# Keys, queries and values read as rows of 6 KB and turned on VectorE; the first two triangular inverses as pairs of 16-blocks; the second group's norms and inverse planned inside the first Mlp

## The chip, the cores and the metric

One NeuronCore of a Trainium2 chip runs the whole program. The metric is the device time of one execution in microseconds. The engines are named as the profile names them: PE (TensorE matmul) and PEld (its weight loads), DVE (VectorE), ACT (ScalarE), POOL (GpSimd) and SP (SyncE, which here only issues DMAs). Every engine runs its own list of instructions strictly in order.

## The reference

A delta-rule attention over 32 heads (batch 4 times 8 heads, 768 tokens, head width 48), then two Mlps over the 3072 tokens, each 384 to 2048 to 384:

```
for t in range(S):                      # 768 steps, for all 32 heads
    y[t]  = q[t] @ state
    v_old = k_n[t] @ state              # k_n = k / (|k| + 1e-6)
    state = state + beta[t] * outer(k_n[t], v[t] - v_old)
x = y as 3072 x 384
x = rational(x @ moe_w_in)  @ moe_w_out     # P(h) / (Q(h) + 1e-6)
x = (h * tanh(softplus(h))) @ moe2_w_out    # h = x @ moe2_w_in
```

## The kernel before, in words

The sequence is cut into 24 chunks of 32 tokens (C = 32), and four chunks make a group (GU = 4), so there are six groups of 128 tokens for each of the 32 heads. One group gives 512 rows of x, which is one column block of the Mlps (TOK = 512).

For each group G the attention has these parts. `norms(G)` loads k of four chunks, squares it (ACT), sums it (DVE), takes the root (ACT, with Ln and Exp) and the reciprocal (DVE). `prepare(u)` scales k of chunk u, transposes k and q on PE, copies them (ACT), forms the Gram matrix (`gram`, PE), and masks it into `lg` (the strictly lower 32 x 32 matrix of each head) and `am`. `inverse(G)` turns the four `lg` tiles with one block transpose (`first`) and then solves for the inverse of a unit triangular 32 x 32 matrix for 128 (chunk, head) pairs at once: for j = 1 to 30 one multiply (L415) and one add (L421), 60 instructions in a row, each needing the one before. Group 0 does this on DVE, groups 1 to 5 on POOL (`ONPOOL`). `finish(G)` transposes the result back (`last`, L440) and scales it by beta into `xt` (L445). `step(u)` then runs the recurrence of chunk u: `ks` (L480), `rest`, `uu` (L492, the first to need `xt`), `s_mm` (L506), `y_mm` (L527), and the transposes that write x.

Each Mlp block (m, G) has 16 units f. A unit is nine matmuls of 512 columns into a bank h (`up`, L751), an activation chain, and nine matmuls into the banks o (`down`, L757). For m = 1 the chain has five DVE instructions (L790 to L796), seven on ACT and two or three on POOL (L785, L789, L798); for m = 2 it is two ACT instructions (Mish) and one on DVE (L802). The weights come as 64-bit floats; `convert` cuts each 384 KB piece to two 32-bit parts, on POOL (clamp L619, and L648 for the low part where kind has "p"), ACT, DVE and, for the first twelve f, on PE (L653, L654).

The order on every engine is made by the class `Plan`: each operation is given with a guessed duration, the buffers that it reads and writes, and a due time; a list scheduler picks, per engine, the ready operation with the earliest latest-start. `early=` moves an attention operation ahead by up to AHEADP = 100000 ns. The plan gets the operations in this order: group 0's attention, norms of group 1, the 16 units (1, 0) with the conversions, then prepares(1), finish(1), norms(2), then in turn the steps of group g + 1, units (2, g), the preparations of group g + 2 and g + 3, and units (1, g + 1).

## Time and profile before

| | us |
|---|---|
| median of 3 runs | 1147.59 (1145.57 to 1147.85) |
| the profiled execution | 1146.76 |
| its span, first to last instruction | 1145.0 |
| PE busy in that span | 1050.4 (92%) |
| DVE / ACT / POOL busy | 630.6 / 613.7 / 571.8 |

The span is the time from the first to the last instruction; 1.8 us of the execution lie around it. A busy share is a mean over stages that differ much: PE is nearly always busy from 452 us on, and it is the first 452 us that hold most of its idle time.

### The profile page before, as it was taken

What the parts mean: (1) busy time and instruction counts of PE and PEld (TensorE: products, weight loads), DVE (VectorE), ACT (ScalarE), POOL (GpSimd) and SP (SyncE); (2) the same over time, 40 slices, a digit from 0 to 9 for tenths busy, and PEclk for the clock granted to TensorE, in tenths of its full rate; (3) what the DMA queues carried; (4) which work ended last, traced back from release to release, by engine and by line L of the source; (5) the groups of instructions that cost most, each with busy time, mean ns of one, the idle gap of its engine ahead of it and who ended that gap; (6) DMA issues with size and microseconds to landing.
All of it is one profiled execution on the core that took longest, in us unless ns stands there. A gap on an engine that the chain in (4) does not pass through costs nothing.

```text
span 1145.0 us, 32730 instructions
## 1 busy us (share of the span) xinstructions
PE 1050.4 (92%) x13568; PEld 847.8 (74%) x13568; DVE 630.6 (55%) x1047; ACT 613.7 (54%) x1089; POOL 571.8 (50%) x741
## 2 busy tenths in 40 slices
PE   4858799569899988999999999999999999999997
PEld 4545587347678877778888788888777788889997
DVE  3784698627768843238762248852347668731211
ACT  2525798524578842248852268842257578742221
POOL 3201497896446996716678026785026457600000
PEclk8869999789999998999999999999999999999999
DMA  7665783737986764657676566766557556766773
GB/s 154 147 190 132 225 286 100 240 111 212 274 250 166 211 183 120 148 146 190 172 207 182 145 166 176 194 169 176 134 159 190 134 153 190 194 179 189 198 207 83
DMA packets 194228, 202.79 MB, mean 177 GB/s; under 512 B 126464, under 2 KB 139776, under 8 KB 194080
## 3 DMA queue, kind: packets, MB, share of 16 engines
q1 hardware_dynamic: 182304, 197.85, 62.8%
q10 hardware_dynamic: 11648, 2.76, 1.3%
q8 instruction: 107, 1.75, 0.7%
q14 instruction: 41, 0.34, 0.1%
q0 software_dynamic: 128, 0.10, 0.0%
HBM read 168.40 MB, written 29.88 MB: 173 GB/s over the span
## 4 chain that ended last, share of the span: by engine, by line
PE 75%; POOL 8%; DVE 5%; DMA 5%; ACT 3%; issue 3%; SPq 1%; ACTq 0%; DVEq 0%; POOLq 0%
PE b_h L751 31%; PE b_o L757 24%; PE b_o L766 4%; PE b_t L527 3%; POOL xs L421 3%; DMA arena<-in_moe_w_in_dram 3%; POOL tmp L415 3%; PE b_t L506 2%; PE b_t L492 2%; PE b_t L361 2%; PE b_t L480 2%; PE b_t L766 1%; PE b_t L349 1%; PE b_h L653 1%; DMA kn<-in_k_dram 1%
## 5 line engine op out<-in xcount | busy, mean ns | idle before, releaser
L751 PE MATMUL b_h<-x,win 128*128 128x512 f32 x1620 | 409.2, 397 | 12.8 <-ACT mq L801 9.7
L751 PEld LDWEIGHTS b_h<-x,win 128*128 128x128 f32 x1620 | 299.1, 189 | 80.3 <-ACT mq L801 10.3
L757 PE MATMUL b_o<-gh,wout 128*128 128x512 f32 x1332 | 335.4, 397 | 5.0 <-POOL wout L648 2.8
L757 PEld LDWEIGHTS b_o<-gh,wout 128*128 128x128 f32 x1332 | 246.2, 189 | 59.7 <-POOL wout L648 3.6
L802 DVE TENSOR_TENSOR gh<-mq,gh 128x512 fp32r<-128x512 f32 x96 | 71.9, 750 | 205.3 <-ACT mq L801 198.1
L800 ACT ACTIVATE gh<-b_h 128x512 fp32r<-128x512 f32 x96 | 57.4, 598 | 216.4 <-PE b_h L751 211.9
L789 POOL TENSOR_TENSOR mq<-mq,mr 128x512 f32<-128x512 f32 x96 | 124.3, 1295 | 79.8 <-ACT mr L787 75.2
L798 POOL TENSOR_TENSOR gh<-mq,gh 128x512 fp32r<-128x512 f32 x96 | 124.3, 1296 | 34.9 <-ACT gh L797 34.5
L421 POOL TENSOR_TENSOR xs<-xs,tmp 128x30 f32<-128x30 f32 (+9 forms) x150 | 84.4, 563 | 11.8
L794 DVE SCALAR_TENSOR_TENSOR mq<-mq,b_r 128x512 f32<-128x512 f32 x96 | 65.6, 683 | 44.7 <-ACT b_r L793 44.5
L790 DVE TENSOR_TENSOR ms<-ms,b_h 128x512 f32<-128x512 f32 x96 | 65.4, 681 | 37.5 <-ACT ms L788 36.8
L415 POOL TENSOR_TENSOR tmp<-xs 128x30 f32<-128x30 f32 (+9 forms) x150 | 78.5, 524 | 9.8
L619 POOL TENSOR_SCALAR arena<-arena 128x384 f32<-128x384 f32 x64 | 34.0, 533 | 98.5 <-PE b_h L653 58.0
L781 ACT ACTIVATE mr<-mq,cst 128x512 f32<-128x512 f32 x96 | 69.1, 720 | 19.2 <-POOL mq L789 18.4
L783 ACT ACTIVATE mq<-b_h 128x512 f32<-128x512 f32 x96 | 56.9, 592 | 41.1 <-PE b_h L751 39.7
L788 ACT ACTIVATE ms<-b_h,ab 128x512 f32<-128x512 f32 x96 | 73.9, 770 | 5.9 <-PE b_h L751 5.4
L791 DVE SCALAR_TENSOR_TENSOR ms<-ms,ab,b_h 128x512 f32<-128x512 f32 x96 | 71.7, 747 | 3.2
L795 DVE SCALAR_TENSOR_TENSOR b_r<-ms,ab,b_r 128x512 f32<-128x512 f32 x96 | 71.9, 749 | 0.0
L797 ACT CAST gh<-mq 128x512 fp32r<-128x512 f32 x96 | 58.8, 615 | 16.2 <-DVE mq L796 13.1
L796 DVE SCALAR_TENSOR_TENSOR mq<-mq,b_r 128x512 f32<-128x512 f32 x96 | 65.7, 685 | 2.5
L793 ACT ACTIVATE b_r<-mr 128x512 f32<-128x512 f32 x96 | 57.7, 601 | 2.8 <-DVE mq L796 1.5
L785 POOL TENSOR_SCALAR mr<-mq,ab 128x512 f32<-128x512 f32 x48 | 37.3, 776 | 40.9 <-ACT mq L783 40.3
(165 smaller groups left out, 1401.0 us busy)
## 6 DMA issues: line engine op xcount, KB each, us to landing
win<-wd SPq DMA_DIRECT2D x164, 384.0 KB
wout<-wd SPq DMA_DIRECT2D x164, 384.0 KB
arena<-in_moe_w_out_dram SPq DMA_DIRECT2D x32, 384.0 KB
wd<-x SPq DMA_DIRECT2D x24, 384.0 KB
wd<-win SPq DMA_DIRECT2D x16, 384.0 KB
wd<-wout SPq DMA_DIRECT2D x16, 384.0 KB
arena<-in_moe_w_in_dram SPq DMA_DIRECT2D x16, 384.0 KB
kn<-in_k_dram SPq DMA_DIRECT2D x88, 48.0 KB
```

What stands on the lines that cost most here:

```text
L415: eng.tensor_tensor(out=tv, in0=row[:, j, j + 1:C].unsqueeze(1).to_broadcast([128, j, n]), in1=xs[:, 0:j, j:j + 1].to_broadcast([128, j, n ...
L421: eng.tensor_tensor(out=xs[:, 0:j, j + 1:C], in0=xs[:, 0:j, j + 1:C], in1=tv, op=ALU.add)
L751: nc.tensor.matmul(out=h, lhsT=win[:, a, j], rhs=x[:, c, slab[j]], start=n == 0, stop=n == 8)
L757: nc.tensor.matmul(out=self.banks[f"o{d}"], lhsT=wout[:, a, d], rhs=gh[:, c], start=first and j == 0, stop=last and j == 2,)
L781: act(out=r, in_=q, func=ACTF.Ln, bias=k["c"])
L788: p.add("ACT", 775, lambda: act(out=s, in_=h, func=ACTF.Identity, scale=k["a3"], bias=k["a2"]), [hb], [sb])
L789: p.add("POOL", 1335, lambda: P.tensor_tensor(out=q, in0=q, in1=r, op=ALU.mult), [rb], [qb])
L791: p.add("DVE", 750, lambda: V.scalar_tensor_tensor(out=s, in0=s, scalar=k["a1"], in1=h, op0=ALU.add, op1=ALU.mult), [hb], [sb])
L795: p.add("DVE", 750, lambda: V.scalar_tensor_tensor(out=rp, in0=s, scalar=k["a0"], in1=rp, op0=ALU.add, op1=ALU.mult), [sb], ["r"])
L796: p.add("DVE", 690, lambda: V.scalar_tensor_tensor(out=q, in0=q, scalar=2.0, in1=rp, op0=ALU.subtract, op1=ALU.mult, reverse0=True), ["r"] ...
L798: p.add("POOL", 1320, lambda: P.tensor_tensor(out=gh[:, 1], in0=q, in1=gh[:, 0].bitcast(F32), op=ALU.subtract), [qb], [ghb])
L802: p.add("DVE", 755, lambda: V.tensor_tensor(out=gh[:, 1], in0=q, in1=gh[:, 0].bitcast(F32), op=ALU.subtract), [qb], [ghb])
```

## The change

- **Loads.** k, q and v of one group were 16 DMAs each, with runs of 192 bytes (one token of one head). They are now rows of 32 tokens (32 x 48 x 4 = 6 KB) of one head: four DMAs for k and q, two for v. The row lands in a staging tile with (head, chunk) on partitions, and one DVE transpose in blocks of 32 x 32 over 1536 columns (`turn`) puts tokens on partitions. There are three such turns per group. The staging tile is the one that holds outputs of the second Mlp (`ev`), and for later groups a part of the arena; k, q and v take it in turn. q and v share one tile, `qv`. The loads of group 0 are all issued by SP but for half of k; before, ACT issued half of k, and q and v.
- **Norms.** k is squared, summed and scaled in the staging tile, in one or two instructions over 1536 columns, before it is turned. The scaling is one instruction per group (DVE for group 0, POOL for the others).
- **Inverse of groups 0 and 1** (`HALVED`): the two diagonal 16 x 16 blocks are solved together in 14 steps (28 instructions of 28 to 112 elements, not 60 of 30 to 240). The lower left block is then added by `finish`: 128 small matmuls (`right`), an ACT copy, 128 small matmuls (`left`) and one DVE instruction, with one more DVE transpose of 512 columns beside them.
- **Place in the plan.** prepares(1), finish(1) and norms(2) are given to the plan at f = 6 of the first Mlp's 16 units, no longer behind them; norms and prepares of groups 3 to 5 at f = 2 of units (1, g + 1).
- **Smaller:** the exchange of k halves between partitions (`swap`) is two DMAs per group, not eight; `mb`, `y`, `kns` and the norm tiles have one buffer; `heat` multiplies the identity by itself; all four `mq` tiles hold q of group 0.

```
+HALVED = (0, 1)
...
+    def load(self, what, G, engines):
+        n = 128 // len(self.src[what])
+        for i, src in enumerate(self.src[what]):
+            engines[i % 2].dma_start(
+                out=self.staging(what, G)[0][n * i:n * i + n], in_=src[:, GU * C * G:GU * C * (G + 1)].rearrange("n (g t) d -> n g (t d)", g=GU)
+            )
+    def staging(self, what, G):
+        return self.stages[G >= (3 if what == "k" else 2)]
+    def turn(self, out, stage):
+        self.nc.vector.transpose(
+            out=out[:, :, :, 0:self.D].rearrange("p g m d -> p d m g"), in_=stage.rearrange("p t d -> p d t")
+        )
...
     def setup(self):
-        for u in range(GU):
-            self.load_k(u, nc.sync, (0, 1))
-            self.load_k(u, nc.scalar, (2, 3))
+        self.load("k", 0, (nc.sync, nc.scalar))
...
     def norms(self, p, G):
+        on, eng, ns = ("POOL", nc.gpsimd, 3300) if G else ("DVE", nc.vector, 1750)
+        p.add(
+            on, ns, lambda: eng.tensor_tensor(
+                out=stage, in0=stage, in1=w["ri"].unsqueeze(2).to_broadcast([128, C, D]), op=ALU.mult
+            ), [f"{wb}r"], staged, early=lead(AHEADX, G),
+        )
+        p.add("DVE", TURN, lambda: self.turn(kg, stage), staged, names, early=lead(AHEADX, G))
...
     def inverse(self, p, G):
+        nb = 2 if G in HALVED else 1
+        L = C // nb
-        for j in range(1, C - 1):
+        for j in range(1, L - 1):
...
     def finish(self, p, G):
+        if G in HALVED:
+            p.add("PE", 2000, right, names + [f"lg{g}" for g in range(GU)], ["t0"], early=lead(AHEADX, G))
+            p.add(
+                "ACT", 600, lambda: nc.scalar.activation(out=low, in_=bank, func=ACTF.Identity, scale=self.half),
+                ["t0"], [lowb], early=lead(AHEADX, G),
+            )
+            p.add("PE", 2000, left, [upb, lowb], ["t0"], early=lead(AHEADX, G))
...
     def first(f):
+        if f == 6:
+            at.prepares(plan, 1)
+            at.finish(plan, 1)
+            at.norms(plan, 2)
...
     units(1, 0, 0, first)
-    at.prepares(plan, 1)
-    at.finish(plan, 1)
-    at.norms(plan, 2)
     for g in range(NG - 2):
...
-        if g + 3 < NG:
-            at.norms(plan, g + 3)
-            at.prepares(plan, g + 3)
-        else:
+        if g + 3 == NG:
             at.steps(plan, g + 2)
-        units(1, g + 1, g + 2 == NG - 1)
+        units(1, g + 1, g + 2 == NG - 1, lambda f: prepare(g + 3) if f == 2 and g + 3 < NG else None)
```

The order of instructions on three engines shows what the plan makes of it.

ACT, from the program's start (L229, L235 and L241 load k, q and v; L303 squares k). Before:

```order
L229 DMA kn_148<-in_k_dram 32x8x48 x8
L892 ACTIVATE minus<-ident_144 128x128
L241 DMA v_151<-in_v_dram 32x8x48 x4
L235 DMA qn_149<-in_q_dram 32x8x48 x4
L303 ACTIVATE sq_171<-kn_148 128x384
```

Now (L234 loads, L340 squares, L354 takes the first half of the root):

```order
L234 DMA ev_134<-in_k_dram 32x1x1536 x2
L986 ACTIVATE minus<-ident_138 128x128
L1003 ACTIVATE ab<-ab 128x2
L340 ACTIVATE kn_142<-ev_134 128x16x48 x2
L717 ACTIVATE arena<-arena 128x384
L354 ACTIVATE nrm_1_167<-nrm_0_166 128x32
```

The loads of v and q have left ACT's list, and the first square stands behind two DMA issues instead of sixteen.

DVE, between the third `lg` of group 0 and the first steps of its inverse (L633 and L638 are weight conversion, L367 writes `lg`, L406 is `first`). Before:

```order
L367 TENSOR_TENSOR lg_172<-b_t_103,mb_165 128x256
L633 TENSOR_SCALAR b_r<-arena 128x384
L638 SCALAR_TENSOR_TENSOR arena<-arena,b_r 128x384
L633 TENSOR_SCALAR b_r<-arena 128x384
L638 SCALAR_TENSOR_TENSOR arena<-arena,b_r 128x384
L367 TENSOR_TENSOR lg_172<-b_t_103,mb_166 128x256
L406 STREAM_TRANSPOSE b_o<-lg_172 128x1024
L409 MEMSET b_o 128x32
```

Now, from the second `lg` on (L413 writes `lg`, L245 is a turn, L726 and L731 are weight conversion):

```order
L413 TENSOR_TENSOR lg_160<-b_t_103,mb_155 128x256
L245 STREAM_TRANSPOSE mq_122<-ev_134 128x48x8x4
L413 TENSOR_TENSOR lg_160<-b_t_103,mb_155 128x256
L726 TENSOR_SCALAR b_r<-arena 128x384
L731 SCALAR_TENSOR_TENSOR arena<-arena,b_r 128x384
L726 TENSOR_SCALAR b_r<-arena 128x384
L731 SCALAR_TENSOR_TENSOR arena<-arena,b_r 128x384
L413 TENSOR_TENSOR lg_160<-b_t_103,mb_155 128x256
L448 STREAM_TRANSPOSE b_o<-lg_160 128x1024
L451 MEMSET b_o 128x32
L453 MEMSET b_o 128x16x16
```

The turn of q stands between the second and the third `lg`; the turn of v stands three steps into the inverse, further down.

POOL, where the inverse of group 1 begins. Before, it comes behind the last L798 of units (1, 0), among the conversions for the second Mlp:

```order
L798 TENSOR_TENSOR gh_133<-mq_126,gh_133 128x512
L648 TENSOR_TENSOR x_114<-arena,x_114 128x384
L648 TENSOR_TENSOR win_115<-arena,win_115 128x384
L619 TENSOR_SCALAR arena<-arena 128x384 x2
L648 TENSOR_TENSOR wout_119<-arena,wout_119 128x384
```

(Eight rows further on in this list, L409 begins it.) Now it stands among the units; L884 and L893 are L789 and L798 of before, and 24 more rows of the inverse follow the four shown, before the next L893:

```order
L893 TENSOR_TENSOR gh_131<-mq_122,gh_131 128x512
L741 TENSOR_TENSOR x_113<-arena,x_113 128x384
L880 TENSOR_SCALAR mr_126<-mq_122,ab 128x512
L884 TENSOR_TENSOR mq_122<-mq_122,mr_126 128x512
L712 TENSOR_SCALAR arena<-arena 128x384
L451 MEMSET xs_161 128x32
L453 MEMSET xs_161 128x16x16
L468 TENSOR_TENSOR tmp_163<-xs_161 128x28
L474 TENSOR_TENSOR xs_161<-xs_161,tmp_163 128x2x14
L468 TENSOR_TENSOR tmp_163<-xs_161 128x52
L474 TENSOR_TENSOR xs_161<-xs_161,tmp_163 128x2x2x13
```

The whole inverse has moved in front of eight of the 16 L893 of units (1, 0).

## Rows read from the trace of the kernel before

**Rows 1.** The page, part 1: busy us (share) and count of each engine.

```profile
PE 1050.4 (92%) x13568; PEld 847.8 (74%) x13568; DVE 630.6 (55%) x1047; ACT 613.7 (54%) x1089; POOL 571.8 (50%) x741
```

**Rows 2.** Windows: us, then busy us of PE, PEld, DVE, ACT, POOL; PEclk, DMA share, GB/s.

```profile
0.00:117.40 117.40, 78.31 (x1967) 60.80 (x1968) 66.54 (x154) 46.52 (x104) 25.16 (x57) 0.84 0.64 158
117.40:205.00 87.60, 79.74 (x581) 62.86 (x580) 74.87 (x128) 72.95 (x136) 66.85 (x69) 0.98 0.67 203
205.00:260.00 55.00, 32.52 (x246) 24.17 (x246) 24.24 (x38) 21.07 (x38) 50.11 (x87) 0.81 0.51 172
260.00:327.00 67.00, 61.36 (x1423) 47.50 (x1421) 48.33 (x91) 37.77 (x78) 32.14 (x43) 1.00 0.82 246
420.00:452.00 32.00, 25.23 (x167) 20.02 (x167) 10.11 (x12) 7.70 (x14) 21.84 (x44) 0.89 0.48 132
452.00:1100.00 648.00, 642.57 (x8111) 523.14 (x8111) 330.23 (x510) 347.91 (x589) 301.58 (x356) 1.00 0.65 173
```

**Rows 3.** Timeline of ACT and its DMA queue (ACTq), opening: start, us, instruction, [idle before].

```profile
13.54 2.90 ACTq L235 DMA_DIRECT2D qn<-in_q_dram  x4
16.49 0.52 ACT L303 ACTIVATE sq<-kn 128x384 f32<-128x384 f32 x1 [9.03 <-DMA arena<-in_moe_w_in_dram]
...
47.36 0.52 ACT L624 ACTIVATE arena<-arena 128x384 f32<-128x384 f32 x1 [4.32 <-DMA mq<-in_q_dram]
```

**Rows 4.** Timeline of DVE, opening: from the scaled k to the inverse's end.

```profile
27.02 1.66 DVE L373 TENSOR_TENSOR kn<-kn,nrm 128x384 f32<-128x384 f32 x2
...
30.91 0.42 DVE L367 TENSOR_TENSOR lg<-b_t,mb 128x256 f32<-128x256 f32 x1
...
43.50 2.03 DVE L406 STREAM_TRANSPOSE b_o<-lg 128x1024 f32<-128x1024 f32 x1
...
48.98 0.18 DVE L415 TENSOR_TENSOR tmp<-xs,b_o 128x30 f32<-128x30 f32 x1
...
50.50 0.27 DVE L415 TENSOR_TENSOR tmp<-xs,b_o 128x108 f32<-128x108 f32 x1
...
72.50 1.89 DVE L440 STREAM_TRANSPOSE xt<-b_o 128x1024 f32<-128x1024 f32 x1
```

**Rows 5.** Timeline of PE: the first matmul on `xt`, and the first `up`.

```profile
74.91 1.34 PE L492 MATMUL b_t<-r,xt 32*32 32x48 f32 x56 [12.87 <-DVE xt L445]
...
117.42 2.22 PE L751 MATMUL b_h<-x,win 128*128 128x512 f32 x9
```

**Rows 6.** Timeline of POOL: first weight piece, and the inverse of group 1.

```profile
13.37 0.53 POOL L619 TENSOR_SCALAR arena<-arena 128x384 f32<-128x384 f32 x1 [2.77 <-DMA arena<-in_moe_w_in_dram]
...
213.17 0.24 POOL L415 TENSOR_TENSOR tmp<-xs 128x30 f32<-128x30 f32 x1
...
215.84 0.40 POOL L421 TENSOR_TENSOR xs<-xs,tmp 128x108 f32<-128x108 f32 x1
```

**Rows 7.** Timeline of PE in the same stretch.

```profile
226.25 3.95 PE L751 MATMUL b_h<-x,win 128*128 128x512 f32 x9 [8.60 <-ACT mq L801]
...
259.88 0.32 PE L492 MATMUL b_t<-r,xt 32*32 32x48 f32 x10
```

**Rows 8.** Groups by line: xcount, busy us, mean ns, idle before and its releasers.

```profile
L445 POOL TENSOR_TENSOR xt<-xt,beta_t 128x256 f32<-128x256 f32 x20 | 13.1, 687 | 85.8 <-DVE xt L440 85.8
L440 DVE STREAM_TRANSPOSE xt<-xs 128x1024 f32<-128x1024 f32 x5 | 11.0, 2203 | 9.2 <-PE b_t L492 6.4 <-POOL xs L421 2.7
L271 DVE STREAM_TRANSPOSE lg<-xs 128x768 f32<-128x768 f32 x1 | 1.0, 978 | 4.5 <-DMA xs<-in_beta_dram 4.5
```

**Rows 9.** Timeline of ACT: table loads of the norms of group 3.

```profile
318.78 1.28 ACT L315 ACT_TABLE_LOAD   x1
```

**Rows 10.** Timeline of PE: the longest wait after 300 us.

```profile
433.07 1.11 PE L349 MATMUL b_t<-ident,kn 128*128 128x128 f32 x4 [6.76 <-DVE lg L367]
```

**Rows 11.** Timeline of SP's queue: the swap of k halves for chunk 1.

```profile
79.50 0.60 SPq L473 DMA_DIRECT2D kns<-kn  x1
87.59 0.60 SPq L474 DMA_DIRECT2D kns<-kn  x1
```

More of the change, by code (lines that the diff above doesn't have):

```diff
@@ L39 @@
 PER_KB = 3.3
+TURN = 3100
 class Plan:
@@ L257, in setup @@
         nc.gpsimd.memset(self.mask_a, 1.0)
+        nc.gpsimd.memset(self.half, 0.0)
+        for e in range(4):
+            nc.gpsimd.memset(self.half[32 * e:32 * e + 16], 1.0)
         for e in range(4):
@@ L290, in steps, with swap @@
     def steps(self, p, G):
+        self.fetch(p, "v", G, lead(AHEAD, G))
+        stage, staged = self.staging("v", G)
+        p.add("DVE", TURN, lambda: self.turn(self.qv, stage), staged, [f"qv{g}" for g in range(GU)], early=lead(AHEAD, G))
+        kg = self.kg[G % 2].rearrange("p g m d -> p (g m) d")[:, :, 0:self.D]
+        kns = self.kns[:, :, 0:self.D]
+        def swap():
+            self.nc.sync.dma_start(out=kns[0:64], in_=kg[64:128, 1::2])
+            self.nc.sync.dma_start(out=kns[64:128], in_=kg[0:64, 0::2])
+        p.dma(1400, 800, swap, [f"kn{(GU * G + g) % self.NKN}" for g in range(GU)], ["kns"], early=lead(AHEAD, G))
         for g in range(GU):
@@ L369, in prepare @@
         if "k" in what:
-            x = kn[:, :, 0:D]
-            on, eng, ns = ("DVE", nc.vector, 480) if u in (0, 2) else ("POOL", nc.gpsimd, 840)
-            p.add(
-                on, ns, lambda: eng.tensor_tensor(
-                    out=x, in0=x, in1=w["ri"][:, g].unsqueeze(2).to_broadcast([128, M, D]), op=ALU.mult
-                ), [f"{wb}r"], [knb], early=lead(AHEADX, G),
-            )
             p.add(
@@ L427, in inverse @@
+        half = 8 // nb
+        for j in range(1, L - 1):
             if G == 0 and j in (1, half):
-                rows = slice(0, half) if j == 1 else slice(half, C)
-                p.add("ACT", 400 if j == 1 else 800, lambda rows=rows: nc.scalar.copy(out=row[:, rows], in_=xs[:, rows]), xb, ["xs"], early=lead(AHEADX, G))
-            n = j * (C - 1 - j)
+                rows = slice(0, half) if j == 1 else slice(half, L)
+                view = lambda t, rows=rows: t.rearrange("p (b j) i -> p b j i", b=nb)[:, :, rows]
+                p.add(
+                    "ACT", 400 if j == 1 else 800, lambda view=view: nc.scalar.copy(out=view(row), in_=view(xs)),
+                    xb, ["xs"], early=lead(AHEADX, G),
+                )
+            n = nb * j * (L - 1 - j)
```

191 lines of the change are left out of this document (117 added, 74 removed).

## The prediction

> **What bounds the kernel now.** I read the page's busy shares first: PE works 1050.4 of 1145.0 us [rows 1], so about 95 us can be won without less matmul work. The windows by stage say where they lie [rows 2]. From 452 to 1100 us PE is busy 642.57 of 648 at clock 1.00: nothing outside PE's own work pays there. Up to 117.4 us, though, PE is busy 78.3 us at clock 0.84, much of it `heat` and weight conversion, and 205 to 260 holds 32.5 busy us of 55 at clock 0.81. Then the timelines, for what ends last in these two places.
>
> The opening is a chain through all engines. ACT can square k only at 16.49, because it still issues the loads of v and q [rows 3]. Then come scaling at 27.02, the first `lg` at 30.91, `first` at 43.50, 60 inverse instructions from 48.98 to 72.50, and L440 [rows 4]. PE gets `xt` at 74.91 after 12.87 us idle, and the first `up` at 117.42 [rows 5].
>
> In 205 to 260 POOL is busy 50.1 of 55 [rows 2] with the inverse of group 1, which starts at 213.17 [rows 6], and which PE sees end at 259.88 with the next `uu` [rows 7]. In between stands an 8.60 us wait of PE for Mish [rows 7].
>
> The sum is made against the profiled execution, 1146.76 us (span 1145.0), which is 0.8 below the median of 1147.59; I carry no correction for that. About 0.2% (2.3 us) is what a measurement of this kernel tells from no change.
>
> **The opening: -13 us (bounds -4 and -18).** With ACT's 16 issues of v and q gone, k is squared as soon as it lands, and something else on DVE is late next: the two DVE instructions of the first weight piece, whose clamp on POOL is at 13.37 [rows 6], stand ahead of the reciprocals. At the price of that clamp (0.53) they end at 14.4. Five tiny DVE instructions, at 0.18 to 0.35 each, 1.4: 15.8. The scaling of 1536 columns: 1.66 for two of 384 makes 0.83 each, 3.3 for four; 0.42 for 256 makes 2.5 [rows 4]. I take 2.5, since one instruction has no start between: 18.3. The turn: no row has this form. L406 takes 2.03 for 1024 columns, L440 1.89 once and 2.203 in the mean, L271 0.978 for 768 [rows 4, 8]. For 1536 columns that is 3.05, 2.8, 3.3 and 1.96. I take 3.05, as the turn writes with strides like the first two: 21.3. From scaled k to the first `lg` 3.9 as now: 25.2 (30.91 now). From there to `first` 12.6 as now, though the turn of q (3.05) stands in it and the masks share one `mb`: conversions behind which it stood cover it. That gives 37.8. From `first` to the first inverse step 5.5 now, of which ACT was held 4.32 by a DMA issue of `mq` [rows 3]; without that 2.03 and a copy of rows, 3.2: 41.0. The inverse: the first six instructions took 1.52 (48.98 to 50.50), 0.25 each, for 30 to 84 columns; the new ones have 28 to 112, so 28 at 0.29 make 8.1. The turn of v within adds 3.05, and the copy 0.5: 52.7. L499 (L440 before) 1.9: 54.6. The correction has no row. 56 small matmuls took 1.34 and ten 0.32 [rows 5, 7], so 128 of them 3.1 to 4.1, or a third of that if 16 columns, not 48, count; two batches, an ACT copy and a DVE instruction (0.5 each, with hand-overs 1.8) make 4 to 10. I take 6: 60.6, and with the scaling by beta (0.42) 61. Against 74.91 that is 14 earlier; I count 13, since the turns of k and q of group 1 (6.1 us of DVE) now stand in the 42.5 us from there to the first `up`, which mostly waits on PE, ACT and conversions. -4 is the case in which conversions set that time, -18 that of the cheap ends.
>
> [...]
>
> [...]
>
> **The first Mlp: +9 us (bounds +5 and +17).** It takes 87.6 us, with PE 79.7, DVE 74.9, ACT 73.0 and POOL 66.9 busy [rows 2]: full on all four. Into it come, on DVE: `first` 2.0, L499 2.2, the half of it for the upper block 1.1, one instruction on a bank 0.75, two more pairs of masks 0.8; the k norm's small work goes ahead of it, -2 or so: +5. On POOL: 28 inverse instructions. The first seven of now lie 2.67 apart in all (213.17 to 215.84, [rows 6]), 0.38 each, and 0.40 for 108 plus a gap is the dearest; 28 by 0.41 make 11.5. With four L445 at 0.687 [rows 8] 14.2, less the k scaling that moves ahead (some 2): +12. PE gets 256 small matmuls, +3. POOL runs in order, so eight L893, which feed `down`, queue behind the whole inverse; PE then lacks `gh`. With one stall of that size (12) and the five buffers of `gh` to soften it, I take 9; 5 if only DVE's work counts, 17 if DVE's and POOL's add.
>
> **From 205 to 260: -24 us (bounds -15 and -29).** The 43 us inverse leaves POOL's list here. What is left on PE is 32.5 us at clock 0.81, 26.3 at full clock; with some 4.7 for the start of Mish, which waits for its table as now, 31 of the 55 stay. -29 if nothing is waited for. -15 if PE keeps its low clock and the 8.2 us before the inverse.
>
> **Tables: -3 us (0 and -5.6).** Norms of groups 3 to 5 now stand within units (1, .), where the table with Ln and Exp is in place; nine loads of 1.28 [rows 9] vanish. In 260 to 327 PE loses 5.6 of 67 [rows 2], and I credit half. In later stages PE covers them already.
>
> **Turns of later groups: +3 us (0 and +12).** Twelve turns at 3.05 are 37 us of DVE, which has 330 busy of 648 [rows 2]; a turn that stands in front of a masking or of L885 delays it by 3.05 at most. I charge one unhidden, and for the upper bound four.
>
> **Nothing:** the swap as two DMAs, `heat` on the identity (no operand awaited), the single `y` and norm buffers, covered by PE's queue. From 420 to 452 the POOL inverse of group 2 with an `lg` behind it costs PE 6.76 [rows 10]; groups 2 to 5 keep 60 instructions, so this stays.
>
> The sum: -13 + 9 - 24 - 3 + 3 = -28; 1146.8 - 28 is about 1119.
>
> **The rivals.** *Conversions pace the opening:* DVE and POOL convert weights all the way to 117, so an early `xt` only waits elsewhere and 4 of 13 stay: 1128. For it: from 74.91 to 117.42 there are 42.5 us for four steps. Against it: PE's 12.87 us wait was for `xt` alone [rows 5]. *The Mlp gives it back:* L893 behind the inverse at full price (+17) and turns at +12 make 1136. For it: all engines above 66 of 87.6 there. *PE is the only bound:* Mlp +5, turns nothing, 205 to 260 -29, and the wait of [rows 10] moved away (-6.8): 1119 - 4 - 3 - 5 - 6.8 is about 1100. For it: the stretch after 452, where PE hides all else. *The other side, a staging queue:* k, q and v of all groups pass one staging tile in turn, and SP issues in order; a load that waits for the turn before it holds the weight fetches behind it. There are some 15 later loads; if each costs PE more than 1.9 us, the 28 us are gone and it ends slower than now; at 3 us each it is 1119 + 45 = 1164. For it: SP does wait that way, L474 came 8 us after L473 [rows 11]. Against it: after 452 us PE stays busy with hundreds of loads in that queue.
>
> **How the numbers follow.** Main case (1110 to 1124) 0.42; conversions pace 0.16; the Mlp gives it back 0.13; PE alone 0.17; the queue 0.08, at more than 2 us a load; gains and prices that just meet 0.04. The range of 8 in 10 runs from 1096 to 1142: from some 4 below PE alone to 6 above the Mlp case; it leaves out the queue, the draw and the ends of the others. Faster by over 0.2%: 0.88, within 0.04, slower 0.08.
>
> **What would show it.** The first `uu` near 61 and the first `up` near 104; turns of about 3 us; the inverse of group 1 on POOL as some 12 us inside the first Mlp, that Mlp longer by about 9 with PE waits on `gh` just behind it; the 55 us stretch at about 31 and PE's clock higher; three L315 groups of table loads gone. The prediction is wrong if there is a first `up` later than 113, a Mlp above 105 us, SP's queue waiting for a turn with PE idle behind it, or new PE waits after 452.

## The result, and the profile after

The changed kernel takes 1157.16 us (median of 6 runs, 1154.39 to 1161.95), against 1147.89 us before in the same comparison: ratio 1.0089, 95% interval 1.0063 to 1.0114. It is slower, and outside the predicted range. Its profiled execution took 1155.55 us, with a span of 1153.8.

Part 1 of its page, to be read beside [rows 1]:

```profile
PE 1061.0 (92%) x14560; PEld 850.6 (74%) x14560; DVE 672.4 (58%) x1017; ACT 604.0 (52%) x1065; POOL 543.2 (47%) x697
```

PE has 10.6 us more to do (although `heat`, the filler matmuls, fell from 20.0 us in 104 rows to 13.4 in 72), and its idle time in the span is about what it was (92.8 us, 94.6 before). What the shorter inverse freed on POOL did not become a shorter span.

I cut both executions at the same events: the first `up`, the last L891 of the first Mlp (L796 before), the first Mish on DVE (L897, L802 before), and the first L891 of units (1, 1). Windows of the changed kernel between them, and the long stretch from 452 us, columns as in [rows 2]:

```profile
0.00:125.90 125.90, 80.34 (x2511) 62.05 (x2512) 69.46 (x129) 49.45 (x106) 25.50 (x59) 0.81 0.60 181
125.90:223.30 97.40, 86.39 (x1147) 66.87 (x1145) 76.25 (x114) 70.92 (x126) 72.33 (x95) 0.95 0.45 140
223.30:242.50 19.20, 11.40 (x34) 7.19 (x34) 16.11 (x27) 12.93 (x22) 14.77 (x18) 0.91 0.79 256
242.50:339.20 96.70, 94.42 (x1625) 74.66 (x1625) 68.58 (x113) 52.47 (x104) 43.01 (x52) 0.98 0.76 250
452.00:1100.00 648.00, 635.54 (x7996) 513.16 (x7995) 351.12 (x510) 338.84 (x572) 302.16 (x363) 1.00 0.62 170
```

The two windows of the kernel before that answer to the third and the fourth:

```profile
199.00:226.20 27.20, 13.56 (x236) 10.30 (x235) 17.29 (x33) 15.99 (x29) 23.52 (x42) 0.81 0.77 241
226.20:341.20 115.00, 99.20 (x1625) 76.24 (x1626) 70.26 (x122) 57.10 (x111) 72.06 (x103) 0.95 0.69 211
```

The account of the two profiled executions closes to the difference of their spans, 8.8 us:

| stretch | before | after | difference | predicted |
|---|---|---|---|---|
| start to the first `up` | 117.4 | 125.9 | +8.5 | -13 |
| first `up` to the last L891 of the first Mlp | 81.5 | 97.4 | +15.8 | +9 |
| from there to the first L891 of units (1, 1) | 142.3 | 115.9 | -26.4 | -24 and -3 |
| from there to the last Mish | 790.2 | 801.0 | +10.9 | +3 |
| last Mish to the end | 13.6 | 13.6 | 0 | 0 |

The third row came as forecast, and the last, for which nothing was counted; the others did not.

**The opening.** DVE of the changed kernel, timeline, at the steps of the prediction's chain:

```profile
17.22 2.80 DVE L245 STREAM_TRANSPOSE kn<-ev 128x1536 f32<-128x1536 f32 x1
...
24.38 0.42 DVE L413 TENSOR_TENSOR lg<-b_t,mb 128x256 f32<-128x256 f32 x1 [1.51 <-PE b_t L407]
...
35.95 2.00 DVE L448 STREAM_TRANSPOSE b_o<-lg 128x1024 f32<-128x1024 f32 x1
...
41.19 0.18 DVE L468 TENSOR_TENSOR tmp<-xs,b_o 128x28 f32<-128x28 f32 x1 [0.22 <-ACT xs L485]
...
46.34 2.80 DVE L245 STREAM_TRANSPOSE qv<-ev 128x1536 f32<-128x1536 f32 x1 [3.70 <-DMA ev<-in_v_dram]
...
55.28 1.89 DVE L499 STREAM_TRANSPOSE xt<-b_o 128x1024 f32<-128x1024 f32 x1
...
71.60 0.75 DVE L542 SCALAR_TENSOR_TENSOR xt<-b_t,half,xt 128x512 f32<-128x512 f32 x1 [8.81 <-PE b_t L526]
```

PE of the same stretch:

```profile
57.23 2.47 PE L519 MATMUL b_t<-xt,lg 32*32 32x16 f32 x169 [12.29 <-DVE xt L499]
62.41 1.37 PE L519 MATMUL b_t<-xt,lg 32*32 32x16 f32 x87 [2.71 <-issue]
...
66.74 1.53 PE L526 MATMUL b_t<-xs 32*16 32x16 f32 x161
70.50 0.94 PE L526 MATMUL b_t<-xs 32*16 32x16 f32 x95 [2.23 <-issue]
...
78.18 0.68 PE L587 MATMUL b_t<-r,xt 32*32 32x48 f32 x26
```

Up to L499 the chain keeps the forecast within 3 us: first `lg` at 24.4 (25.2 forecast), `first` at 35.95 (37.8), first inverse step at 41.2 (41.0), end of the inverse at 55.3 (52.7, since the turn of v waits 3.70 us for its load). Then the correction takes 15.2 us (57.2 to 72.35) where 6 were counted. Each batch is 256 rows of the trace, not 128 (169 and 87, 161 and 95). The matmuls of both batches take 6.3 us, the two pauses within them 4.9, and `heat` and weight conversion that the plan put between them 3.0. ACT's copy for the correction (L532) starts at 65.98, not at 63.78, where the first batch ends: ACT's list has the square of group 1's k ahead of it, which waited 14.53 us for its load:

```profile
64.19 1.48 ACT L340 ACTIVATE kn<-ev 128x1536 f32<-128x1536 f32 x1 [14.53 <-DMA ev<-in_k_dram]
```

Behind the correction stands `ks` in PE's list, long done at this point in the kernel before, so `uu` comes 5.4 us after `xt` is ready. At 78.18 it is 3.3 us later than in [rows 5], not 14 earlier. From there to the first `up` it takes 47.7 us, where it took 42.5. Windows of these two stretches, first of before and then of after:

```profile
74.91:117.42 42.51, 36.40 (x1360) 28.14 (x1360) 20.55 (x41) 22.55 (x51) 5.37 (x10) 0.90 0.50 124
```

```profile
78.18:125.90 47.72, 38.08 (x1423) 29.26 (x1423) 21.35 (x40) 22.42 (x52) 8.02 (x11) 0.89 0.57 185
```

Within neither of them does the profile show PE waiting for another engine or for a DMA. PE works, and the rest (6.1 us before, 9.4 after) are pauses that the profile puts to "issue": time in which PE waited for nothing that it shows.

**The first Mlp.** The window of before that answers to the second one of the changed kernel, and PE's longest wait in the latter (what it waited for: total us, times, longest):

```profile
117.40:198.90 81.50, 74.09 (x499) 58.64 (x497) 69.17 (x115) 69.27 (x129) 61.91 (x62) 0.98 0.67 205
```

```profile
PE b_o L852 <- POOL gh L893: 3.3, 2, 2.7
```

Of the 15.8 us, 12.3 are work of PE (86.4 busy, 74.1 before). 6.3 of them are the two batches of group 1's correction, and the same 128 rows of `down` take 3.2 more (34.6, 31.4 before), with the granted clock at 0.76 between 192 and 213 us.

**Between the two Mlps.** SP's queue, timeline:

```profile
188.65 0.38 SPq L700 DMA_DIRECT2D arena<-in_moe_w_in_dram  x1
205.84 3.08 SPq L234 DMA_DIRECT2D ev<-in_k_dram  x4
```

SP's waits from 150 to 260 us (what it waited for: total us, times, longest), and the window of the wait:

```profile
SPq L234 <- PE b_t L526: 10.9, 1, 10.9
SPq L234 <- DVE ev L536: 5.9, 1, 5.9
```

```profile
180.00:205.00 25.00, 19.29 (x491) 14.57 (x491) 18.23 (x26) 14.79 (x25) 21.87 (x40) 0.86 0.11 34
```

The load of k of group 2 stands at the head of SP's list for 16.8 us, because the staging tile also holds the work tiles of group 1's correction, and the DMA share falls to 0.11. That is the staging queue of the last rival, at one load and not at fifteen: SP's other waits for a load of k, q or v lasted 5.0 us at most.

**After 339 us.** One block of units (1, .) and the stretch behind it, windows, first of before and then of after:

```profile
522.86:598.22 75.36, 75.36 (x759) 60.97 (x758) 58.82 (x94) 57.24 (x96) 54.61 (x62) 1.00 0.72 189
598.22:687.49 89.27, 88.68 (x1428) 70.73 (x1428) 28.34 (x47) 34.42 (x59) 34.98 (x53) 1.00 0.63 166
```

```profile
521.88:595.52 73.64, 71.15 (x502) 56.53 (x495) 63.11 (x95) 55.88 (x94) 48.91 (x42) 1.00 0.71 194
595.52:692.94 97.42, 95.03 (x1691) 75.10 (x1690) 33.70 (x46) 32.58 (x57) 38.01 (x69) 1.00 0.54 151
```

Before, PE is busy in the block without a gap. After, it loses 2.5 us in it, DVE has 4.3 us more to do there, and PE's instructions in the block fall from 759 to 502; they are done in the next stretch, which is 8 us longer. The whole of it, from the first L891 of units (1, 1) to the last Mish, as windows, and what PE waited for in them (total us, times, longest), first before and then after:

```profile
341.20:1131.40 790.20, 778.00 (x9207) 634.82 (x9206) 405.56 (x624) 423.76 (x717) 389.10 (x479) 1.00 0.65 172
PE b_t L349 <- DVE lg L367: 6.8, 1, 6.8
PE b_h L751 <- DVE ms L791: 1.1, 2, 0.6
```

```profile
339.20:1140.20 801.00, 781.26 (x9205) 632.91 (x9206) 440.26 (x636) 417.32 (x707) 387.64 (x475) 1.00 0.62 171
PE b_h L846 <- DVE ms L886: 7.4, 9, 1.6
PE b_o L852 <- POOL gh L893: 2.4, 6, 0.6
```

Of the 10.8 us between these windows, 3.3 are work of PE and 7.5 idle time. The one long wait of [rows 10] is gone, and many short ones for DVE's `ms` and POOL's `gh` have come, both of units (1, .).

### The profile page after: what moved, and what is told of

It is laid out like the page before. It is cut to its first block, busy times and chain, and to the rows that moved or that the text cites. A ratio compares the mean times of both kernels' runs of the same rounds, so it can differ in the third digit from the quotient of the medians.

```text
span 1153.8 us, 34301 instructions
## 1 busy us (share of the span) xinstructions
PE 1061.0 (92%) x14560; PEld 850.6 (74%) x14560; DVE 672.4 (58%) x1017; ACT 604.0 (52%) x1065; POOL 543.2 (47%) x697
## 4 chain that ended last, share of the span: by engine, by line
PE 60%; DVE 5%; ACT 5%; POOL 4%; DMA 3%; issue 2%; SPq 1%; DVEq 0%; POOLq 0%; ACTq 0%
PE b_h L846 25%; PE b_o L852 19%; PE b_o L861 4%; PE b_t L622 3%; PE b_t L601 2%; PE b_t L587 1%; PE b_t L861 1%; POOL xs L474 1%; POOL tmp L468 1%; PE b_t L575 1%; DMA wd<-win 1%; DMA arena<-in_q_dram 1%; POOL mq L884 1%; DVE mq L889 1%; DVE b_r L890 1%
## 5 line engine op out<-in xcount | busy, mean ns | idle before, releaser
L852 PEld LDWEIGHTS b_o<-gh,wout 128*128 128x128 f32 x1332 | 246.0, 189 | 63.4 <-POOL gh L893 10.3
L884 POOL TENSOR_TENSOR mq<-mq,mr 128x512 f32<-128x512 f32 x96 | 124.2, 1294 | 108.2 <-ACT mr L882 104.8
L897 DVE TENSOR_TENSOR gh<-mq,gh 128x512 fp32r<-128x512 f32 x96 | 72.5, 755 | 163.0 <-ACT mq L896 162.8
L893 POOL TENSOR_TENSOR gh<-mq,gh 128x512 fp32r<-128x512 f32 x96 | 124.1, 1293 | 56.3 <-ACT gh L892 55.4
L878 ACT ACTIVATE mq<-b_h 128x512 f32<-128x512 f32 x96 | 56.8, 591 | 42.9 <-PE b_h L846 37.7
L468 POOL TENSOR_TENSOR tmp<-xs 128x58 f32<-128x58 f32 (+9 forms) x134 | 70.1, 523 | 9.7
L474 POOL TENSOR_TENSOR xs<-xs,tmp 128x58 f32<-128x58 f32 (+9 forms) x134 | 68.3, 510 | 10.5
L891 DVE SCALAR_TENSOR_TENSOR mq<-mq,b_r 128x512 f32<-128x512 f32 x96 | 65.8, 686 | 2.8
L896 ACT ACTIVATE mq<-b_h 128x512 f32<-128x512 f32 x96 | 56.9, 593 | 0.0
```

The source lines that it names most:

```text
L468: eng.tensor_tensor(out=tv, in0=part(row, slice(j, j + 1), slice(j + 1, L)).to_broadcast([128, nb, j, n]), in1=part(xs, slice(0, j), slice ...
L474: eng.tensor_tensor(out=to, in0=to, in1=tv, op=ALU.add)
L852: nc.tensor.matmul(out=self.banks[f"o{d}"], lhsT=wout[:, a, d], rhs=gh[:, c], start=first and j == 0, stop=last and j == 2,)
L884: p.add("POOL", 1335, lambda: P.tensor_tensor(out=q, in0=q, in1=r, op=ALU.mult), [rb], [qb])
L893: p.add("POOL", 1320, lambda: P.tensor_tensor(out=gh[:, 1], in0=q, in1=gh[:, 0].bitcast(F32), op=ALU.subtract), [qb], [ghb])
L897: p.add("DVE", 755, lambda: V.tensor_tensor(out=gh[:, 1], in0=q, in1=gh[:, 0].bitcast(F32), op=ALU.subtract), [qb], [ghb])
```

## The experiments

Sixteen kernels, each with 4 to 12 executions. The times are medians, the ratios those to the kernel before in the same comparison. The other columns are read from each run's own profiled execution: first `uu` and first `up` on PE, the last L891 of the first Mlp, the first Mish on DVE, the first L891 of units (1, 1), and the time from that to the last Mish.

```
run                     us      ratio (95%)               uu    up     Mlp ends  Mish   (1,1)   to last Mish
before                  1147.9  1                         74.9  117.4  198.9     226.2  341.2   790.2
after                   1157.2  1.0089 (1.0063-1.0114)    78.2  125.9  223.3     242.5  339.2   801.0
e1_full0                1159.3  1.0092 (1.0068-1.0115)    70.9  122.2  223.9     240.5  335.7   803.0
e2_place_late           1158.0  1.0090 (1.0067-1.0113)    79.2  125.8  223.0     242.5  342.2   802.9
e3_f2_late              1166.9  1.0169 (1.0150-1.0189)    79.0  125.0  220.9     239.8  350.3   801.9
e4_direct_later         1156.9  1.0086 (1.0066-1.0107)    77.7  127.0  223.2     242.5  340.0   801.0
e5_nocorr0              1153.1  1.0038 (1.0019-1.0057)    60.4  120.3  222.0     238.5  334.4   801.5
e6_v0_direct            1154.1  1.0054 (1.0035-1.0073)    75.7  124.9  222.1     238.7  335.1   803.1
e7_ev_free              1173.2  1.0209 (1.0176-1.0243)    77.2  128.1  210.2     234.5  346.0   815.9
e8_mb2                  1163.7  1.0145 (1.0117-1.0173)    78.0  126.6  222.8     241.9  337.1   810.9
e9_before_halved1       1141.5  0.9939 (0.9919-0.9959)    76.5  119.1  198.6     220.2  333.6   792.2
e10_before_1buf         1149.8  1.0008 (0.9994-1.0022)    74.7  118.0  201.2     227.8  342.4   790.3
e11_rows_off            1152.8  1.0026 (1.0008-1.0045)    78.9  125.6  223.3     242.5  337.7   799.4
e12_before_halved       1150.1  1.0012 (0.9991-1.0033)    78.0  122.7  204.6     223.0  346.5   789.8
e13_before_halved_f2    1158.2  1.0081 (1.0053-1.0109)    76.1  122.0  205.0     223.4  351.9   795.6
e14_before_halved_sp    1153.8  1.0049 (1.0030-1.0068)    67.3  122.8  202.8     220.6  348.9   792.3
e15_rows_off_place      1148.8  1.0015 (0.9997-1.0034)    77.4  125.4  222.8     243.0  341.6   794.2
e16_rows_off_place_v0   1141.9  0.9951 (0.9933-0.9968)    79.5  130.0  226.2     242.8  338.8   789.9
```

A profile is one execution, and executions of one kernel lie some 4 us to either side of the median, so columns that differ by 2 or 3 us tell nothing.

**e1_full0.**

```
-HALVED = (0, 1)
+HALVED = (1,)
```

> Edit to the changed kernel (1157.2): HALVED = (1,), so group 0's inverse has its 60 instructions again and no correction by small matmuls. Theory A (the opening lost its gain to the correction: 256 matmul instructions for each of its two batches where 128 were counted, and the turn of v inside the inverse): first starts near 36 as now, the 60 instructions and the turn of v end near 68, the first uu comes near 71 and not 78, the first up near 119 and not 126, and the time falls by 5 to 8 us, to about 1150. Rival (conversions set the time of the first up, whatever the inverse does): the first up stays near 126 and the time near 1157.

The first `uu` came at 70.9 as expected, the first `up` only 3.7 us earlier, at 122.2, and the time did not fall. The rival is the nearer: 7 us at `uu` bring next to nothing. Nor does less work of PE by itself: without these batches PE's busy time is 1051.5 us, back at that of before (1050.4).

**e2_place_late.**

```
     def first(f):
...
-        if f == 6:
-            at.prepares(plan, 1)
-            at.finish(plan, 1)
-            at.norms(plan, 2)
...
     units(1, 0, 0, first)
+    at.prepares(plan, 1)
+    at.finish(plan, 1)
+    at.norms(plan, 2)
```

> Edit to the changed kernel: prepares(1), finish(1) and norms(2) are given to the plan behind the first Mlp's 16 units again; all else stays. Theory A (moving group 1's inverse into the first Mlp costs 16 us there, but gives back 27 between the first Mlp and the block (1,1)): the first Mlp falls from 97 to about 82 us, the stretch behind it grows by 20 or more, and the time comes out at 1157 to 1168. Rival (the full first Mlp is where the gain was lost): the time falls by 10 or more, to 1147 or less, since the 16-block inverse is short enough to stand behind the Mlp.

This told neither: the plan gives the same order on all five engines as for the changed kernel, so the run is a second timing of it (1158.0). The place f = 6 in the code is not what brought the inverse into the first Mlp. Nor is its length: in e9 and e12 the 28 instructions start at 240.0 and 236.8, behind the first Mlp. In e7, where only the work tiles of the correction lie elsewhere, they start at 235.1. So it is the staging tile, which the correction has to leave before k of group 2 can be loaded.

**e3_f2_late.**

```
+        if g + 3 < NG:
+            prepare(g + 3)
...
-        units(1, g + 1, g + 2 == NG - 1, lambda f: prepare(g + 3) if f == 2 and g + 3 < NG else None)
+        units(1, g + 1, g + 2 == NG - 1)
```

> Edit to the changed kernel: norms and prepares of groups 3 to 5 stand behind finish(g + 2) again, not at f = 2 of units (1, g + 1). After 598 us the changed kernel loses 11 us against the one before. Theory A (the turns on DVE, 3.1 us each, in units (1, .) do it): the loss stays, three table switches come back, 1157 to 1161. Rival (the new place does it, since more attention work falls into the units): the loss goes, 1146 to 1149.

Slower by almost 10 us, more than either expected. The loss after units (1, 1) begin stayed (801.9), so the place alone is not its cause, and 11 us more were lost ahead of it.

**e4_direct_later** (with a function that issues the 16 DMAs of the kernel before into `qv`).

```
+DIRECTQ = (2, 3, 4, 5)
+DIRECTV = (2, 3, 4, 5)
...
+        for g in range(GU):
+            p.dma(2250, 200, lambda g=g: go(g), (), [f"qv{g}"], early=early)
```

> Edit to the changed kernel: q and v of groups 2 to 5 are loaded straight into their tile as 16 DMAs with runs of 192 bytes, as before the change, so that eight turns (25 us of DVE) vanish; k keeps its 6 KB rows and its turn. Theory A (turns cost the 11 us after 598): the time falls by 6 to 11, to 1146 to 1151. Rival (place of norms and prepares, or the single tile for q and v, does it): within 3 us of 1157. A third: the small runs burden the DMA queues again and it grows above 1160.

No change, and 801.0 in the last column. The turns of q and v alone are not the cause.

**e5_nocorr0.**

```
-        if G in HALVED:
+        if G in HALVED and G:
             rows = self.xs.rearrange("p a b -> p (a b)")
```

> Edit to the changed kernel (1157.2): group 0's correction is left out (the two batches of small matmuls, the ACT copy, the transpose and the DVE instruction), so that the lower left 16 x 16 block of its inverses is missing; group 1 keeps its correction. If the correction is what ate the opening's gain: xt is ready near 58, not 73, the first up comes near 112, not 126, and the time falls by 10 or more, to below 1147. Rival (weight conversions set the time of the first up): the first uu comes 14 us earlier, but the first up at 121 or later, and the time stays within 4 of 1157.

The stretch from the first `uu` of this run to its first `up`, as a window, and PE's one wait for another engine in it:

```profile
60.44:120.30 59.86, 44.00 (x1493) 32.38 (x1494) 28.45 (x49) 26.92 (x60) 9.24 (x13) 0.80 0.56 175
PE b_h L747 <- ACT x L738: 6.3, 1, 6.3
```

`uu` is 17.7 us earlier, where the prediction wanted it, and 12 of these are lost by the first `up`, 60 us later. The time falls by 4.1, between the two expectations and at the rival's edge. Against the changed kernel PE has 5.9 us more to do in this stretch: matmuls that stood ahead of `uu` now stand behind it (26 rows of conversion, L746, where there were 20, and 64 more of `gram`), at a granted clock of 0.80 (0.89). The other 6.3 us are the wait for L738, which stands on ACT behind the square of group 1's k (L340, from 67.84, after 16.37 us of waiting).

**e6_v0_direct.**

```
+DIRECTV = (0,)
```

> Edit to the changed kernel: v of group 0 is loaded straight into its tile by 16 DMAs on SP, without the staging tile, so that its turn (2.8 us) and the 3.7 us wait for its load leave the middle of the first inverse. If the opening's chain through the inverse counts: xt 6 us earlier, the first up near 120, time 1151 to 1153. Rival (conversions set the first up; SP's queue gets 16 more issues ahead of weight pieces): 1156 or more.

2.5 us at `uu`, 1.0 at `up`, which is within the scatter, and 3.1 in the time: between the two expectations, and at most half of the chain's 6.5.

**e7_ev_free.**

```
-            upper, low = (rows[:, 0:512], rows[:, 512:]) if G == 0 else (self.spare2[:, 0], self.spare2[:, 1])
+            upper, low = (rows[:, 0:512] if G == 0 else self.lg.rearrange("p u m t -> p (u m t)")[:, 0:512]), rows[:, 512:]
```

> Edit to the changed kernel: the two work tiles of group 1's correction lie in lg and in the lower half of xs, no longer in the staging tile, so that the k load of group 2 does not wait for the correction. Theory B (SP's list is in order, the k load waits there 16.8 us from 189 to 206, all weight fetches behind it, and the second Mlp's weights come late): SP's wait goes, the next weight piece is clamped near 195, not 216, the first Mish comes near 232, not 242, and the time falls by 5 to 10, to 1147 to 1152. Rival (the full first Mlp, not SP, holds PE in 180 to 240): the first Mish within 3 us of 242, time within 3 of 1157.

SP's 16.8 us wait went, the first Mish came 8 us earlier, and yet the time rose by 16. The edit did more than it should: with the staging tile free, the plan put the load and norms of group 2 into the first Mlp, and the inverse of group 1 (235.1 to 247.8) and its correction (to 266.1) behind it. The price of SP's wait by itself therefore stays open. But the first Mlp without group 1's inverse took 82.1 us (128.1 to 210.2), as before (81.5): the 15.8 us are this inverse and its correction, placed there.

**e8_mb2.**

```
-        mb, mbb = self.mb[0], "mb"
+        mb, mbb = (self.mb[0], "mb") if u % 2 == 0 else (self.tmp.rearrange("p (m t) -> p m t", m=M), "tmp")
```

> Edit to the changed kernel (1157): the mask tile mb has two buffers again (the second lies in tmp, which only the inverse uses). From 339 us on the changed kernel loses 11 us against the one before; POOL waits 28.5 us there for DVE to read mb (7.6 before). Theory C (POOL, in order, holds L884 and L893 of the units behind such a mask): the POOL wait falls below 10, PE's small waits in units (1, .) go, and the time falls by 4 to 8. Rival (POOL has the slack): within 2 of 1157.

POOL's wait for `mb` fell from 28.5 to 14.2 us, and the time rose by 6.5. Theory C is not borne out: the wait fell by half, not below 10, and more freedom at this place was no gain under this plan.

**e9_before_halved1.** The kernel before, with `inverse` and `HALVED = (1,)` of the change. As it ran, the correction is left out (`finish` is that of before), so the time is that of the short inverse alone.

```
+HALVED = (1,)
...
+        nb = 2 if G in HALVED else 1
+        L = C // nb
...
-        for j in range(1, C - 1):
+        for j in range(1, L - 1):
```

> The kernel before (1147.6) with one part of the change: group 1's inverse as two 16-blocks, its two correction tiles in lg and xs; loads, norms, buffers and places stay. Theory (the shorter inverse is worth its price, and the loads, turns and single buffers are where the change loses): the 43 us inverse behind the first Mlp becomes 12 to 15 with 6 us of small matmuls on PE, and the time falls by 8 to 15, to 1133 to 1140. Rival (the weight conversions of the second Mlp hold the stretch behind the first Mlp anyway): within 3 of 1147.6.

6 to 7 us won, not 24: the first Mish comes 6 us earlier and units (1, 1) 7.7. This is what group 1's short inverse gave in the old kernel with nothing paid for it. The plan starts it only at 240.0 (213.2 before), so the next `uu` on PE comes at 258.81, hardly earlier than in [rows 7].

**e10_before_1buf.**

```
-        self.mb = ring("mb", 2, [128, M, C])
+        self.mb = ring("mb", 1, [128, M, C])
...
-        self.y = ring("y", 2, [128, M * D])
+        self.y = ring("y", 1, [128, M * D])
```

> The kernel before with one part of the change: mb and y have one buffer each. Theory C (the single buffers make a part of the 11 us lost after 339): slower by 4 to 8, to 1152 to 1156. Rival (they are covered, as the prediction had it): within 2 of 1147.6.

The single `mb` and `y` cost nothing that can be told.

**e11_rows_off** (e4, and norms that load and scale k by chunk).

```
+DIRECTK = (3, 4, 5)
...
+        if G in DIRECTK:
+            return self.norms_direct(p, G)
```

> Edit to the changed kernel (1157): q and v of groups 2 to 5 and k of groups 3 to 5 are loaded straight into their tiles as before the change, k is squared, summed and scaled chunk by chunk, and no turn is left behind group 2's k; the places at f = 2, the single buffers and the halved inverses stay. If the work that rows and turns bring to DVE and POOL in units (1, .) costs the 11 us after 339 us (each of these blocks loses 2.5 to 4.6 us of PE, where before had none): PE is full in units (1, .) again and the time falls by 7 to 11, to 1146 to 1150. Rival (the place at f = 2, or the single tile for q and v, does it): within 3 of 1157.

4.4 us below the changed kernel, about half of the loss, though its last column is only 1.6 lower. Its second block of units (1, .), a window:

```profile
520.57:597.16 76.59, 75.12 (x642) 60.06 (x635) 60.45 (x96) 57.38 (x97) 50.12 (x46) 1.00 0.71 184
```

PE loses 1.5 us in it, not 2.5, and DVE has 2.7 us less.

**e12_before_halved.** As e9, with the correction.

```
+            p.add("PE", 2000, right, names + [f"lg{g}" for g in range(GU)], ["t0"], early=lead(AHEADX, G))
...
+            p.add("PE", 2000, left, upb + lowb, ["t0"], early=lead(AHEADX, G))
```

> The kernel before (1147.6) with group 1's inverse as two 16-blocks and with its correction, the correction's tiles in lg and xs (the run before this one on the same idea had the short inverse without the correction and gave 1141.5). The correction adds 6 us of small matmuls to PE between the first Mlp and the next steps, where PE has waits to hide a part: 1142 to 1146. Rival (it stands on the path in full): 1147 to 1150, no gain.

The run with the correction of one group takes 8.6 us more than e9, more than the short inverse gave. Not all of it is the correction: the guessed duration of one instruction differs too (420, not 350, for the scaling by beta on DVE), the orders differ from the opening on, and in the profiled executions 3.6 us are lost by the first `up`, where group 1's correction does not yet stand.

**e13_before_halved_f2.**

```
-        units(1, g + 1, g + 2 == NG - 1)
+        units(1, g + 1, g + 2 == NG - 1, lambda f: prepare(g + 3) if f == 2 and g + 3 < NG else None)
```

> The run e12_before_halved with norms and prepares of groups 3 to 5 at f = 2 of units (1, g + 1), with loads, norms and buffers of the kernel before. If the place is harmless and saves nine table loads: 2 to 5 below e12. Rival (attention work in units (1, .) makes PE wait for DVE there, whatever the form of the loads): 4 to 10 above e12.

8.1 us above e12, the rival's size. In the old layout the place at f = 2 is a price, not a saving. In the two profiled executions, 11.1 us apart, 5.4 arise ahead of the first L891 of units (1, 1) and 5.8 behind it. Its second block of units (1, .):

```profile
535.44:612.26 76.82, 74.75 (x700) 59.94 (x693) 60.96 (x98) 56.83 (x96) 54.42 (x60) 1.00 0.72 180
```

PE loses 2.1 us here, without a single turn in the kernel. From units (1, 1) on its waits for DVE's `ms` are 4.6 us, 1.8 in e12.

**e14_before_halved_sp.**

```
-lambda: self.load_q(u, None if G else nc.scalar), (), [qnb], early=lead(AHEADP, G), engine="SP" if G else "ACT")
+lambda: self.load_q(u), (), [qnb], early=lead(AHEADP, G))
```

> The run e12_before_halved with q of group 0 issued by SP, not ACT. ACT squares k 3 us or more earlier and is not held 4 us before the first inverse, so the first uu comes 5 to 8 us earlier. If the chain to the first uu sets the first up: 4 to 7 below e12. Rival (conversions set the first up, as the run without the first correction had it): the first up within 3 us of 117, time within 3 of e12.

The first `uu` is 10.7 us earlier than in e12, the first `up` not at all (122.8, 122.7), and the time is not shorter but 3.7 longer. Between the two events PE has 3.8 us more to do than in e12 and waits 5.8 for conversion copies of ACT. After e1 and e5 it is the third run to say so, in the other kernel.

**e15_rows_off_place** (the edits of e11 and e3 together).

> The run e11_rows_off with norms and prepares of groups 3 to 5 behind finish(g + 2) again, as before the change; what stays of the change is the opening, the halved inverses and the single buffers. In the kernel before with the halved inverse the place at f = 2 cost 8 us (1158.2 against 1150.1). If place and rows are the two causes of the 11 us after 339, the stretch from the start of units (1, 1) to the end is 790 again and the time falls 6 to 9 below e11's 1152.8, to 1144 to 1147. Rival (the single buffers or the single tile for q and v cost it too, or the place only pays or costs together with rows): 1151 to 1154.

4.0 below e11 and 8.4 below the changed kernel, between the two expectations. The last column falls to 794.2, which is 6.8 of the 10.9 lost there. Rows with turns and the place at f = 2 together make up most of what was lost against the kernel before. Undone alone, the rows gave 4.4 (e11), the turns of q and v nothing (e4), and the place the wrong sign (e3). PE's waits for `ms` from units (1, 1) on go the same way: 7.4 us in the changed kernel, 5.2 in e4, 3.2 in e11, 1.1 here and before, but 10.3 in e3.

**e16_rows_off_place_v0.**

```
-DIRECTV = (2, 3, 4, 5)
+DIRECTV = (0, 2, 3, 4, 5)
```

> As e15_rows_off_place, and v of group 0 is loaded straight into its tile too. Alone this edit gave 3 us (1154.1 against 1157.2). If the two add: 3 below e15. Rival (the first up is set by conversions, so it gives nothing): within 2 of e15.

1141.9, 0.49% below the kernel before, the fastest of the study that computes the whole reference. Its second block of units (1, .) and the stretch behind it are nearly those of before again:

```profile
517.72:593.53 75.81, 75.21 (x759) 61.08 (x758) 58.96 (x94) 57.12 (x96) 55.65 (x64) 1.00 0.72 188
593.53:683.03 89.50, 88.66 (x1428) 70.76 (x1428) 28.72 (x47) 34.41 (x59) 33.42 (x51) 1.00 0.64 165
```

Its gain over e15 (6.9 us) is not where its edit is: its first `up`, at 130.0, is the latest of all. It comes from another order behind that, and why this order is better stays open. PE's busy time is 1061.1 us, that of the changed kernel; its idle time is 81.1, not 92.8.

## Why the prediction was wrong

**The opening (-13 forecast, +8.5).** The step that failed is "the 42.5 us from there to the first `up`", taken as fixed behind the first `uu`, so that 13 of the 14 us at `uu` were carried to the first `up`. In e5, e14, e1, before, after and e16 the first `uu` lay at 60.4, 67.3, 70.9, 74.9, 78.2 and 79.5, and the first `up` at 120.3, 122.8, 122.2, 117.4, 125.9 and 130.0. The runs show that an earlier inverse does not bring an earlier first `up` of the same size. The traces show what fills the time instead: PE's own list, 36.4 of the 42.5 us before and 38.1 of 47.7 after, and pauses put to "issue". When `uu` came earlier, PE had more to do behind it (5.9 us in e5 against the changed kernel, where matmuls that had stood ahead of it now stood behind it, and 3.8 in e14 against e12), and a wait for ACT came in (6.3 and 5.8 us); in e5 the granted clock of the stretch was lower as well (0.80, 0.89 in the changed kernel). The rival "conversions pace the opening", with 0.16, had the outcome, and its mechanism only in part: PE does not wait for weight pieces between the two events, before or after; their matmuls are a part of what it has to do (L746, 10.6 us after). No run changed their number, so what they cost is not measured.

The term ahead of it was wrong as well: "I take 6" for the correction, which took 15.2. The matmuls of the two batches are 6.3 of that; the sum had nothing for the pauses within them (4.9) and for what the plan puts between them (3.0), nor for `ks` behind them. Its price for one matmul came from a line that ends at the edge of a window. The whole `uu` of [rows 5], 32 calls, is 64 rows:

```profile
74.91 1.50 PE L492 MATMUL b_t<-r,xt 32*32 32x48 f32 x64 [12.87 <-DVE xt L445]
```

At this price 128 calls are 6.0 us, not 3.1. A smaller slip: the first weight piece has two DVE instructions behind its clamp, and 14.4 counts one.

**The first Mlp (+9 forecast, +15.8).** The size was within the bounds of +5 and +17, but not by the mechanism. The step that failed is the stall ("one stall of that size (12)", of PE behind the eight L893), and with it "PE gets 256 small matmuls, +3". POOL runs the inverse from 180.1 to 191.8 with L893 behind it, and PE waited 3.3 us for it. In place of the stall PE got 12.3 us more to do, of which the two batches are 6.3. On DVE and POOL the sum was near (+7.1 and +10.4 busy, +5 and +12 forecast). That the whole is due to this inverse and its correction in this place is shown by e7, where the Mlp without them took 82.1.

**From 205 to 260, with the tables (-27 forecast, -26.4 to units (1, 1)).** The sum held, but not as a gain. Alone in the old kernel, where the plan started it later, the short inverse gave 6 to 7 us (e9), and with its correction none (e12). In the changed kernel it had moved into the first Mlp, so that Mlp's loss and this stretch's gain belong together: 10.6 net, before the opening's loss.

**Turns of later groups, and tables (+3 and -3 forecast, +10.9 behind units (1, 1)).** The step that failed is the tables' term, which saw only a saving in the place at f = 2. Nine table loads did vanish (27 before, 18 after), but the place puts attention work into units (1, .), where PE had no idle time to lose (75.36 us busy of 75.36 in a block of before). In the old kernel that costs 8.1 us (e13), about half of it behind the start of units (1, 1). The turns' term, "I charge one unhidden", is not shown to be too low by itself: eight turns less gave nothing (e4). The rest of the norms is not more work than before (1.74 us for one reduction on DVE, where four of 0.55 stood, and 2.77 for one scaling on POOL, where four of 0.91 stood), but longer instructions at another place. With rows and place together undone 8.4 come back (e15), and PE's waits for `ms` are those of before. "This stays", of the 6.76 of [rows 10], was wrong the other way: 2.7 are left of it.

**The correction as a whole.** Groups of the changed kernel by line, PE:

```profile
L519 PE MATMUL b_t<-xt,lg 32*32 32x16 f32 x512 | 7.7, 210 | 15.2 <-DVE xt L499 12.3 <-issue 3.0
L526 PE MATMUL b_t<-xs 32*16 32x16 f32 x256 | 2.5, 184 | 2.2 <-issue 2.2
L526 PE MATMUL b_t<-ev 32*16 32x16 f32 x256 | 2.4, 176 | 0.9 <-issue 0.9
```

These 12.6 us are more than the growth of PE's busy time (10.6), but they are not its price in time. Leaving group 0's out took PE's busy time back to 1051.5 and 1050.4 and gave nothing in e1, with the long inverse, and 4.1 us in e5; adding group 1's to the old kernel cost up to 8.6 (e12 against e9). And e16 has both and is faster than the kernel before.

**The staging queue (0.08)** came true at one load, with 16.8 us of SP; its price in time was not separated (e7). Whether it has a part in the slower time is therefore not shown. **Nothing for the single buffers** was right for `mb` and `y` (e10).

What stays open: why e3 loses 11 us ahead of units (1, 1), why e16's order is better than e15's, and whether `heat`, with 72 rows for 104, has a part in the lower granted clock of the opening (0.81, 0.84 before), which no run separates. The plan orders all engines anew after each edit, so an edit of one line is not one change on the chip.

## What to carry to other kernels

Where one engine is the bound for most of the span, price first what a change adds to that engine: in the first Mlp the sum had 3 us for PE, which got 12.3, and a stall of 12, which was 3.3. Before crediting an earlier event, look at what the engine behind it still has to do until the event that counts, and where a wait moves to; a run that leaves the long step out shows it at once, as e5 did. A line at the edge of a window may be cut by it; read its count against the code. And with a list scheduler, compare the orders of instructions ahead of the times: one edit came out as no change at all (e2), another as many (e7).
